# A gated mix of linear attention and a GLU in one kernel: the order of ScalarE's and VectorE's work, denominators in pairs, weight loads behind one another

## The chip, the cores and the metric

One core of a Trainium2 chip runs the whole kernel. The metric is the device time of one execution in microseconds (us); lower is better. TensorE multiplies matrices, ScalarE (ACT in the profile) and VectorE (DVE) work on tiles in SBUF and PSUM, GpSimd (POOL) only issues transfers here, mostly stores, and SyncE (SP) issues all loads. Each of these engines works its own queue of instructions strictly in order: an instruction that waits holds all that stand behind it.

## The reference

```python
def reference(A_x, A_wqkv, A_wo, B_x, B_w_gate, B_w_up, B_w_down, gate_w):
    # x: 2048 tokens x 640, fp32; 32 heads of 20; 1536 features in the GLU
    qkv = (x @ wqkv).reshape(B, S, 3, H, Dh)...
    phi = lambda t: jnp.where(t > 0, t + 1, jnp.exp(t)) + 1e-6
    pq, pk = phi(q), phi(k)
    kv = einsum("bhsd,bhse->bhde", pk, v);  z = einsum("bhsd->bhd", pk)
    num = einsum("bhqd,bhde->bhqe", pq, kv)
    den = einsum("bhqd,bhd->bhq", pq, z) + 1e-6
    a = (num / den).reshape(B, S, D) @ wo
    h = sigmoid(x @ w_gate) * (x @ w_up)
    b = h @ w_down
    g = sigmoid((x * gate_w).sum(-1))
    return g * a + (1 - g) * b
```

All inputs and outputs are fp32.

## The kernel before

**Products.** Every fp32 operand is held as a high and a low part (`split`: ScalarE copies the high part, VectorE subtracts it for the low one), and `mm3` (L214 to L216) issues three matmuls for one product, most of them 128x128 by 128x512. The helpers through which nearly all of ScalarE's and VectorE's work goes have one line each: `act` L225, `vec2` L229, `vec3` L233. So a row of the profile is told apart by its tiles.

**Stages.** First come keys and values, summed over all tokens (0 to about 144 us), then the heads' matrices (`kv_part`, `m_part`) and phi(q) for the second half of the tokens (`q_phase(1)`, to about 206). `f_phase(1)` runs the GLU's twelve feature blocks, f = 0 to 11, for the second half (to 442.5). `q_phase(0)` and `f_phase(0)` do the same for the first half (to about 742). An output stage follows, in which numerators, gate and the parts from the GLU meet (to the end). Blocks of two by two are multiplied with seven products in place of eight (`Block`, steps s1 to s7). The sums of weights this needs are made once, in the second half, on VectorE from a staged tile wst (`queue_g`, `queue_s`, L1052 to L1098), split into wg, wu and ws, stored to DRAM by POOL (`store_w`, L943) and loaded again in the first half by SP (`load_form`, L1018). Some steps start from a product that is already there: a seed, ScalarE's copy of a tile ch in PSUM into a tile dd, after which TensorE adds to dd.

**What sets the order.** The program is written out by hand, with a planner, `Order`. It keeps clocks in us for TensorE, ScalarE and VectorE (`order.pe`, `order.act`, `order.vec`), which each helper moves on by a price: for ScalarE `a_cost(w)` and for VectorE `v_cost(w)`, w the columns of a tile. Work that has no fixed place is put in lists (`order.add`, with prices, a key, a time `ready` before which it isn't taken, and a rank: first, plain, lazy, chain or spare). `fill`, called between products, takes what `_fits`: an item whose end, by the planner's clocks, isn't later than TensorE's clock by more than a slack (0.6 us ScalarE, 1.2 VectorE; 1.6 and 2.4 in q_phase). `order.need(key)` forces an item. The clocks decide only where an instruction stands in its engine's queue; on the chip semaphores make it wait. `W_AT` says when a staged weight is taken to have landed. In `s_part` ws is split in two pieces, each of which needs its part of `sums`.

**Denominators.** phi(q), weighted, is stored by POOL to p_dram while q is made (L1160). `queue_den(g)` (L1196 to L1247) treats one group g of 512 tokens: SP loads five tiles pden (L1208), VectorE sums them with weights zcol into fac (L233), POOL stores the sum (L1218), SP loads it turned (L1224) and the gate's values gs (L1226), VectorE adds twice, takes the reciprocal (L1234) and multiplies by gs, POOL stores the factor (L1236), and SP loads it turned back (L1241). VectorE scales numerators by fac in the output stage, groups 2 and 3 first, then 0 and 1; the scaled tile hf is split into pq for TensorE.

**The GLU's second product.** Two feature blocks make a pair p. Its h is brought into seven forms (B11, B12, B21, B22, T1 to T4; `tail_s` and `queue_h` order them), and multiplied by forms of w_down. Those are made in the second half (`queue_d`, `queue_ds`, `queue_df`) and come back in the first half as one tile wf of 2304 KB, loaded in three pieces (`load_wf`, L1425), wf's tile being single.

**Tiles.** `c_tile` and `h_tile` give out tiles from rings, by turn: "c" tiles, "cx" tiles (which come out of the ring t of four), hf tiles of three pools. A tile given out again makes its new writer wait for the last reader, a store included.

The functions that the change touches follow.

Of the kernel before, what the change touches and what calls it, by code (L numbers as in the profile page):

```python
# [29 lines left out]
class Order:  # L30
# [25 lines left out]
    def follow(self, v, fn, key=None):  # L56

        self.soon.append((self.act, v, fn, key))
# [28 lines left out]
    def _fits(self, it):  # L87
        a, v, fn, key, ready = it
        if ready is not None and self.pe < ready():
            return False  # L90
        end_a = self.act + a
        end = max(self.vec, end_a if a else 0.0) + v
        return not ((a and end_a > self.pe + self.slack_a) or (v and end > self.pe + self.slack_v))
# [64 lines left out]
    def _after(self, after):  # L158
        t = 0.0
        if "p" in after:  # L160
            self.fill()
            t = self.pe
        if "a" in after:
            t = max(t, self.act)
        if "v" in after:
            t = max(t, self.vec)
# [12 lines left out]

def v_cost(w):  # L180
    return 0.155 + w * 0.00104

@with_exitstack
def gated_mix_kernel(ctx: ExitStack, tc: tile.TileContext, xt, xn, wk, wv, wo, wst_q, wst_f, out_t):
# [57 lines left out]
    def split(hi, lo, src, after=""):  # L242
        act(hi, src, AF.Copy, after)
        at = order.act
# [18 lines left out]
    gs = common.tile([P, P], F32, name="gs")  # L263
# [12 lines left out]
    common.tile([P, 64], F32, name="space")  # L276

# [6 lines left out]
    xst = kp.tile([P, 2, KC, CW], F32, name="xst")  # L284

# [419 lines left out]
    def k_split(i, after=""):  # L705
        r = KR.pop(i)
        ph, pl = op_tile("pkh"), op_tile("pkl")
        vh, vl = (t[:, :D].rearrange(view2, j=2) for t in (ph, pl))
        act(vh, r, AF.Copy, after, bias=EPS)
        at = order.act  # L710
# [127 lines left out]
    for c in range(1, 4):  # L838
# [135 lines left out]
        for u in range(2 * KC):  # L974
            g.part(u, 2 if u in g.ps else 0, 4)
            order.fill()
            if u in (3, 5, 7, 9,):
                order.run("qw")
# [21 lines left out]

    def tt(name, dt=F32, shape=(P, TG)):
        return pw.tile(list(shape), dt, name=name, tag="t", bufs=4)
# [19 lines left out]
    WST, W_AT = {}, {}  # L1022
# [173 lines left out]
    def queue_den(g, place=None):  # L1196

        st = {}
        td = fac[:, g]

        def load(u):
            if u < KC:
                if not place:
                    st[u] = tt("pden")
                elif u % 2 == 0:
                    t = place(F32)
                    st[u], st[u + 1] = t[:, 0], t[:, 1]
                nc.sync.dma_start(st[u], p_dram[:, u, g])  # L1208
                st["at", u] = max(order.pe, order.vec) + 9.0

        def one(u):
            if u == 0:
                vec1(td, st[u], zcol[:, 0:1], zeps[:, 0:1], OP.mult, OP.add)
            else:
                vec3(td, st[u], zcol[:, u:u + 1], td, OP.mult, OP.add)
            load(u + 2)
            if u == KC - 1:
                nc.gpsimd.dma_start(den_dram[:, g], td)  # L1218
                st["at", u + 1] = max(order.pe, order.vec) + 7.0

        def turn_in():
            for j in range(4):
                js = slice(j * H, (j + 1) * H)
                nc.sync.dma_start(td[js].rearrange("h (d c) -> h d c", c=P),  # L1224
                                  den_dram[:, g, j * P:(j + 1) * P].rearrange("(d h) c -> h d c", h=H))
            nc.sync.dma_start(gs, gate_rep[4 * g:4 * g + 4].rearrange("i h c -> (i h) c"))  # L1226
            st["at", KC + 1] = max(order.pe, order.vec) + 7.0

        def factor():
# [5 lines left out]
            vec2(q, q, gs, OP.mult)  # L1235
            nc.gpsimd.dma_start(fac_dram[:, g], q)  # L1236
            st["at", KC + 2] = max(order.pe, order.vec) + 7.0

        def turn_out():
            for d in range(4):  # L1240
                nc.sync.dma_start(td[d * H:(d + 1) * H].rearrange("h (j c) -> h j c", c=P),  # L1241
                                  fac_dram[:, g].rearrange("(j h) c -> h j c", h=H))
        order.add(0, 0, lambda: [load(0), load(1)], chain=True)
        for u in range(KC):
            order.add(0, v_cost(TG), lambda u=u: one(u), None, lambda u=u: st["at", u], chain=True)
        for n, (v, fn) in enumerate(((0, turn_in), (2.0, factor), (0, turn_out))):
            order.add(0, v, fn, ("fac", g) if n == 2 else None, lambda n=n: st["at", KC + n], chain=True)  # L1247
# [108 lines left out]
    def load_d():  # L1356
        if d_loads:
# [3 lines left out]
            DST[n] = (t, order.pe + 4.0)  # L1361
# [15 lines left out]
    def queue_ds(p):  # L1377
# [16 lines left out]
        for part in range(2):  # L1394
            order.add(0, 2 * v_cost(2 * P), lambda part=part: sums(part), lazy=True)

    def queue_df(p):
# [16 lines left out]
        for j in range(2):  # L1414
            order.add(a_cost(w), v_cost(w), lambda j=j: forms(j), ("ds", p), lazy=True)
# [4 lines left out]
    def load_wf(p):  # L1420
# [3 lines left out]
        for c0, c1 in ((0, D), (D, 2 * D), (2 * D, WF)):  # L1424
# [17 lines left out]
    def queue_d(n):  # L1442
        if not down_pool:
# [3 lines left out]
                  lazy=True)  # L1447
# [86 lines left out]
    def h_tile(dt=F32R):  # L1534

        i, last = 0, 4
        if "h" in turn:
            last = 3 if "c" in turn else 4
            i = (turn["h"] % 8 >= 4) + (turn["h"] % 8 >= 4 + last)
            turn["h"] += 1  # L1540
        return down_pool[i].tile([P, 2, TG], dt, name="hf", tag=f"hf{i}", bufs=(4, last, 1)[i])
# [40 lines left out]
    def tail_s(f, blk):  # L1582
# [17 lines left out]
        def t5():  # L1600
# [123 lines left out]
    def q_phase(pr, b12, extra):  # L1724
# [9 lines left out]
        for j, (u, b) in enumerate(steps):  # L1734
            if isinstance(u, Block):
# [23 lines left out]
                if pr:  # L1759
# [7 lines left out]
                    elif blk is A and s == 6:  # L1767
                        queue_g(("f", pr, 0))
                    elif blk is A and s == 7:
                        queue_s(("f", pr, 0))  # L1770
                else:
# [19 lines left out]
    dens = ({0: 2, 2: 3, 4: 0, 6: 1}, {})  # L1791

    def f_phase(pr, q, hooks={}):
# [3 lines left out]
        if pr:  # L1797
            turn.update(c1=0, c22=0, h=0)

        def step(f, s):  # L1800
# [6 lines left out]
            if pr and s == 1:  # L1807
                order.need(("w", n, 0), False)
# [22 lines left out]
            if pr:  # L1831
                if s == 7 and f + 2 < FC:
                    queue_s(("f", pr, f + 2))
                if s == 2 and f + 1 < FC:
                    queue_g(("f", pr, f + 1))
                    if f == 0:
                        queue_s(("f", pr, 1))
# [4 lines left out]
        next(q, None)  # L1842
        step(0, 1)
# [3 lines left out]
        for f in range(FC):  # L1847
            if f % 2:
                order.need(("h", f // 2 - 1, "T3"), False)
            down = iter(())  # L1850
            if f % 2 and f > 1:
# [11 lines left out]
            for s in (3, 4, 5):  # L1863
                step(f, s)
                next(down, None)
                if pr and s == 4:
                    if f < 2 or f % 2:
                        queue_d(("f", 1, f))
                    if f % 2 and f < FC - 1:
                        queue_ds(f // 2)  # L1870
            if f + 1 < FC:
# [5 lines left out]
            if f % 2 and f < FC - 1:  # L1877
                if not pr and f > 1:
                    load_wf(f // 2)
                queue_t1(f // 2)  # L1880
                if pr:
                    queue_df(f // 2)
# [4 lines left out]
            if f in dens[pr]:  # L1887
                queue_den(dens[pr][f])
            step(f, 7)
        if pr:  # L1890
# [46 lines left out]
    extra[13].append(lambda: order.need(("w", ("f", 1, 0), 0), False))  # L1937
    for hg, (j, t) in enumerate(((1, "rot"), (2, "rot"), (3, "dd"), (5, "rot"), (6, "rot"), (8, "rot"))):
# [421 lines left out]
```

## Time and profile before

| | before |
|---|---|
| three executions | 803.31, 803.03, 801.63 us |
| median | 803.03 us |
| the profiled execution | 808.18 us, of which the span is 806.0 |
| mean granted TensorE clock | 0.972 |
| moved by DMA | 173.53 MB, mean 215 GB/s |

The profile comes from one execution of its own, 5.2 us above the median, and its rows are held against its own time. "busy" counts from an instruction's start to its end; successive instructions of one engine overlap, so the distance from start to start (the pitch) is shorter than the duration. "[1.51 <-ACT dd L225]" says that the engine stood idle 1.51 us ahead of that instruction, and that ScalarE's writing of dd ended the idle time. PEclk is the share of its full clock that TensorE was granted. A DMA row gives the time of its issue on the queue, and "us to landing" the median from issue to landing.

### The profile page before, as it was taken

The page shows a single profiled execution, that of the slowest core. Times are in us where ns is not written, and L with a number is a line of the kernel's source. Part 1 is how long each engine was busy: PE and PEld are TensorE (multiplying, and loading weights), DVE is VectorE, ACT ScalarE, POOL GpSimd, SP SyncE. Part 2 cuts the span into 40 slices and gives each one's busy share as a digit, 9 for nine tenths or more (in the row PEclk, how much of TensorE's full clock was granted, in tenths as well). Part 3 has the DMA queues.
Part 4 walks back from the last instruction along what each step waited for, and adds up shares of the span by engine and source line. Part 5 has one row for each costly group of instructions (what it writes and reads, how often), then busy time and mean ns, then how long its engine had stood idle before and what let it go on. Part 6 is the DMA issues. An engine that isn't in the chain of part 4 may idle for free.

```text
span 806.0 us, 10081 instructions
## 1 busy us (share of the span) xinstructions
PE 750.3 (93%) x3575; PEld 628.8 (78%) x3575; DVE 568.2 (71%) x987; ACT 357.8 (44%) x661; POOL 94.6 (12%) x161
## 2 busy tenths in 40 slices
PE   9999999997989899988988999999999899998398
PEld 8999999785776777766766888888888688886276
DVE  5978879785676887878869832636767466894496
ACT  6665474476447543434354454354142314231251
POOL 0220201032112110111110210000001300000000
PEclk9999999998999999999999999999999899999589
DMA  7564566985856745554846558849785947494212
GB/s 267 133 186 112 150 182 162 279 295 181 313 191 238 284 156 197 229 208 173 344 177 251 182 196 314 317 149 347 252 325 180 266 174 301 167 349 145 85 65 93
DMA packets 71000, 173.53 MB, mean 215 GB/s; under 512 B 11642, under 2 KB 32394, under 8 KB 67238
## 3 DMA queue, kind: packets, MB, share of 16 engines
q1 hardware_dynamic: 54582, 109.99, 41.2%
q0 software_dynamic: 16224, 62.74, 21.8%
q8 instruction: 28, 0.46, 0.2%
q14 instruction: 22, 0.18, 0.1%
q10 hardware_dynamic: 144, 0.16, 0.1%
HBM read 103.96 MB, written 63.92 MB: 208 GB/s over the span
## 4 chain that ended last, share of the span: by engine, by line
PE 64%; DVE 11%; DMA 10%; issue 9%; ACT 4%; SPq 1%; POOL 1%; DVEq 0%; POOLq 0%; ACTq 0%
PE ch L214 6%; PE ch L216 6%; PE ch L215 6%; PE cc L216 6%; PE cc L215 5%; PE cc L214 5%; PE dd L214 5%; PE dd L216 5%; PE dd L215 5%; PE rot L214 4%; PE rot L215 4%; PE rot L216 4%; DMA ws<-wf 2%; DVE tb L229 1%; DVE hf L229 1%
## 5 line engine op out<-in xcount | busy, mean ns | idle before, releaser
L229 DVE TENSOR_TENSOR hf<-c,hf 128x512 fp32r<-128x512 f32 x74 | 50.7, 689 | 48.9 <-ACT hf L225 47.8
L225 ACT ACTIVATE c<-ch 128x512 f32<-128x512 f32 x50 | 29.8, 595 | 98.6 <-PE ch L216 98.5
L225 ACT ACTIVATE hf<-c 128x512 fp32r<-128x512 f32 x74 | 46.0, 626 | 48.5 <-DVE c L229 48.2
L214 PE MATMUL ch<-xth,ws 128*128 128x512 f32 x112 | 44.8, 400 | 7.0 <-DMA ws<-wf 3.9
L229 DVE TENSOR_TENSOR c<-cc,c 128x512 f32<-128x512 f32 x38 | 26.2, 690 | 35.2 <-PE cc L216 18.5
L214 PE MATMUL dd<-xrh,wg 128*128 128x512 f32 x90 | 36.3, 403 | 12.6 <-ACT dd L225 12.6
L216 PE MATMUL ch<-xth,ws 128*128 128x512 f32 x112 | 44.6, 398 | 0.0
L215 PE MATMUL ch<-xtl,ws 128*128 128x512 f32 x112 | 44.5, 398 | 0.0
L229 DVE TENSOR_TENSOR tb<-rot,tb 128x512 f32<-128x512 f32 (+1 forms) x59 | 38.2, 676 | 6.3 <-PE rot L216 5.4
L229 DVE TENSOR_TENSOR tb<-dd,tb 128x512 f32<-128x512 f32 x44 | 30.2, 687 | 13.4 <-PE dd L216 13.3
L216 PE MATMUL dd<-xrh,wg 128*128 128x512 f32 x90 | 35.9, 399 | 0.0
L215 PE MATMUL dd<-xrl,wg 128*128 128x512 f32 x90 | 35.7, 397 | 0.0
L214 PE MATMUL cc<-xbh,ws 128*128 128x512 f32 x84 | 33.5, 399 | 0.0
L215 PE MATMUL cc<-xbl,ws 128*128 128x512 f32 x84 | 33.3, 396 | 0.0
L216 PE MATMUL cc<-xbh,ws 128*128 128x512 f32 x84 | 33.2, 395 | 0.0
L229 DVE TENSOR_TENSOR c<-c,c 128x512 f32<-128x512 f32 x44 | 30.1, 685 | 2.4 <-ACT c L225 2.0
L214 PE MATMUL rot<-pkh,xnh 128*128 128x320 f32 x102 | 31.6, 310 | 0.0
L215 PE MATMUL rot<-pkl,xnh 128*128 128x320 f32 x102 | 31.5, 309 | 0.0
L214 PEld LDWEIGHTS dd<-xrh,wg 128*128 128x128 f32 x90 | 17.1, 190 | 18.5 <-ACT dd L225 15.1
L216 PE MATMUL rot<-pkh,xnl 128*128 128x320 f32 x102 | 31.5, 308 | 0.0
L225 ACT ACTIVATE ws<-wst 128x640 fp32r<-128x640 f32 (+1 forms) x26 | 17.4, 679 | 30.7 <-DVE wst L229 17.9
L214 PEld LDWEIGHTS ch<-xth,ws 128*128 128x128 f32 x112 | 21.4, 191 | 12.2 <-DMA ws<-wf 4.3
(649 smaller groups left out, 2341.7 us busy)
## 6 DMA issues: line engine op xcount, KB each, us to landing
wf<-ws POOLq DMA_DIRECT2D x12, 1152.0 KB, 7.5
ws<-wf SPq DMA_DIRECT2D x12, 1152.0 KB, 8.2
wst<-wst_f SPq DMA_DIRECT2D x12, 640.0 KB, 6.9
wf<-wg POOLq DMA_DIRECT2D x12, 640.0 KB, 7.5
wd<-wd POOLq DMA_DIRECT2D x12, 640.0 KB, 7.7
wg<-wf SPq DMA_DIRECT2D x12, 640.0 KB, 4.0
wf<-wd SPq DMA_DIRECT2D x10, 640.0 KB, 5.8
xnst<-xn SPq DMA_DIRECT2D x16, 320.0 KB, 4.5
```

Of the source, the lines that this page charges most:

```text
L214: nc.tensor.matmul(out, l_hi, r_hi, start=first, stop=False, skip_group_check=True)
L215: nc.tensor.matmul(out, l_hi, r_lo, start=False, stop=False, skip_group_check=True)
L216: nc.tensor.matmul(out, l_lo, r_hi, start=False, stop=last, skip_group_check=True)
L225: nc.scalar.activation(out, src, fn, **kw)
L229: nc.vector.tensor_tensor(out, a, b, op=op)
```

## The change

The program keeps its instructions: ScalarE, VectorE, SP, POOL and TensorE have as many as before, and TensorE's matmuls stand in the same order, but for the PSUM banks of the last batch of GT. What differs is where the others' instructions stand in their queues, and which tiles some of them use.

1. Prices: one for ScalarE and one for VectorE, lower than before, and lags of 0.2, 0.18 and 0.14 us where one engine reads what TensorE, ScalarE or VectorE wrote.

```diff
-        self.act = max(self.act, t) + 0.19 + w * 0.00084
+        self.act = max(self.act, t) + a_cost(w)
...
-        self.vec = max(self.vec, t) + 0.155 + w * 0.00104 * rate
+        self.vec = max(self.vec, t) + v_cost(w * rate)
+
+P_LAG, A_LAG, V_LAG = 0.2, 0.18, 0.14
 
 def a_cost(w):
-    return 0.19 + w * 0.00084
+    return 0.06 + w / 1200
 
 def v_cost(w):
-    return 0.155 + w * 0.00104
+    return 0.07 + w / 960
```

2. The split of ws isn't taken before its sums are through by VectorE's clock, and the weights of f + 1 are queued a step or more earlier (`queue_g` and `queue_s` of f = 0 and 1 within `q_phase`), and forced at step 7 of the block before.

```diff
+            SUM_AT[n, 1 - part] = order.vec + V_LAG
...
+            order.act = max(order.act, SUM_AT[n, part])
             split(h[:, cs], l[:, cs], WST[n][:, part, :cut[part + 1] - cut[part]])
...
-                order.add(a_cost(w), v_cost(w), lambda part=part: s_part(part), ("w", n, part))
+                order.add(a_cost(w), v_cost(w), lambda part=part: s_part(part), ("w", n, part),
+                          lambda part=part: SUM_AT.get((n, part), 1e9))
...
-            if pr and s == 1:
-                order.need(("w", n, 0), False)
+            if pr and s == 7 and f + 1 < FC:
+                for part in range(2):
+                    order.need(("w", ("f", 1, f + 1), part), False)
```

3. Denominators of two groups together, item by item in turn: groups 2 and 3 from f = 3 of `f_phase(0)` on, groups 0 and 1 from f = 7. Each group's gs has a tile of ring t. The work per group is the same.

```diff
-    dens = ({0: 2, 2: 3, 4: 0, 6: 1}, {})
+    dens = ({3: (2, 3), 7: (0, 1)}, {})
...
-    def queue_den(g, place=None):
+    def queue_dens(*gs2):
...
+        order.add(0, 0, lambda: [load(g, u) for u in range(2) for g in gs2], chain=True)
         for u in range(KC):
-            order.add(0, v_cost(TG), lambda u=u: one(u), None, lambda u=u: st["at", u], chain=True)
+            for g in gs2:
+                order.add(0, v_cost(TG), lambda g=g, u=u: one(g, u), None, lambda g=g, u=u: st["at", g, u], chain=True)
```

4. `load_wf(f // 2)` moves from behind step 1 of the next block to behind step 7, which puts it behind that step's load of ws on SP's queue; its pieces come in another order, the one that is used first in front.

```diff
-        for c0, c1 in ((0, D), (D, 2 * D), (2 * D, WF)):
+        for c0, c1 in ((D, 2 * D), (0, D), (2 * D, WF)):
...
-                if not pr and f > 1:
-                    load_wf(f // 2)
                 queue_t1(f // 2)
...
             step(f, 7)
+            if not pr and f % 2 and 1 < f < FC - 1:
+                load_wf(f // 2)
```

5. Forms of h: B22 is queued first, and T3 = B22 - B12 is made behind it; T4 and T3 are queued only at step 3 of the next odd block. The turns c1, c22 and h begin in `f_phase(1)` after q_phase's first step there in place of ahead of it, so that `q_phase(1)` takes "c" tiles where it took "cx" tiles. The last hf tile of eight comes from another pool.

```diff
-        if pr:
-            turn.update(c1=0, c22=0, h=0)
...
         next(q, None)
+        if pr:
+            turn.update(c1=0, c22=0, h=0)
         step(0, 1)
...
-            queue_h(p, "B22")
-            queue_h(p, "T4")
-            HR[p, "T3"] = t3 = HR.pop((p, "B12"))
-            queue_h(p, "T3", lambda: sub(t3, HR[p, "B22"], t3))
+            HR[p, "T3"] = t3 = HR[p, "B22"]
+            b12 = HR.pop((p, "B12"))
+
+            def b22():
+                h_form(p, "B22")
+                order.then(lambda: sub(t3, t3, b12))
+            order.add(a_cost(TG), 2 * v_cost(TG), b22, ("h", p, "B22"), first=True)
...
+                if s == 3 and f % 2 and f > 1:
+                    queue_h(f // 2 - 1, "T4")
+                    queue_h(f // 2 - 1, "T3")
```

6. Smaller: the first w_down forms are no longer lazy (`lazy=p > 0`, `lazy=n[2] > 1`), `DST`'s landing is taken at 10 us in place of 4, and the last GT batch takes the banks rot, dd, rot, cc in turn.

More of the change, by code (lines that the diff above doesn't have):

```diff
@@ L243, in split @@
         act(hi, src, AF.Copy, after)
-        at = order.act
+        at = order.act + A_LAG
         def low():
@@ L709, in k_split @@
         act(vh, r, AF.Copy, after, bias=EPS)
-        at = order.act
+        at = order.act + A_LAG
         def low():
@@ L999, in gated_mix_kernel @@
     pw2 = pw2_cm.__enter__()
+    pw2.tile([P, 2, D], F32, name="wst", tag="wst", bufs=2)
+    pw2.tile([P, 2, TG], F32R, name="hf", tag="hf2")
+    pw2.tile([P, 256], F32, name="room")
     def tt(name, dt=F32, shape=(P, TG)):
@@ L1194, in gate_store, with load, one, turn_in @@
         nc.sync.dma_start(gate_rep, gate_dram[0].rearrange("(i o p) -> i o p", o=1, p=P).broadcast_to([n, H, P]))
[L1196 removed]
+    def queue_dens(*gs2):
         st = {}
[L1199 to L1201 removed]
+        def load(g, u):
             if u < KC:
[L1203 to L1211, printed above, removed]
+                st[g, u] = tt("pden")
+                nc.sync.dma_start(st[g, u], p_dram[:, u, g])
+                st["at", g, u] = max(order.pe, order.vec) + 9.0
+        def one(g, u):
+            td = fac[:, g]
             if u == 0:
[L1213 removed]
+                vec1(td, st[g, u], zcol[:, 0:1], zeps[:, 0:1], OP.mult, OP.add)
             else:
[L1215 to L1216 removed]
+                vec3(td, st[g, u], zcol[:, u:u + 1], td, OP.mult, OP.add)
+            load(g, u + 2)
             if u == KC - 1:
                 nc.gpsimd.dma_start(den_dram[:, g], td)
[L1219 to L1221 removed]
+                st["at", g, u + 1] = max(order.pe, order.vec) + 7.0
+        def turn_in(g):
             for j in range(4):
                 js = slice(j * H, (j + 1) * H)
[L1224 removed]
+                nc.sync.dma_start(fac[js, g].rearrange("h (d c) -> h d c", c=P),
                                   den_dram[:, g, j * P:(j + 1) * P].rearrange("(d h) c -> h d c", h=H))
[L1226 to L1229 removed]
+            st[g, "gs"] = tt("gs")[:, :P]
+            nc.sync.dma_start(st[g, "gs"], gate_rep[4 * g:4 * g + 4].rearrange("i h c -> (i h) c"))
+            st["at", g, KC + 1] = max(order.pe, order.vec) + 7.0
+        def factor(g):
+            td = fac[:, g]
             q = td[:, :P]
@@ L1394, in queue_ds @@
         for part in range(2):
-            order.add(0, 2 * v_cost(2 * P), lambda part=part: sums(part), lazy=True)
+            order.add(0, 2 * v_cost(2 * P), lambda part=part: sums(part), lazy=p > 0)
     def queue_df(p):
@@ L1534, in h_tile @@
     def h_tile(dt=F32R):
-        i, last = 0, 4
+        i = 0
         if "h" in turn:
-            last = 3 if "c" in turn else 4
-            i = (turn["h"] % 8 >= 4) + (turn["h"] % 8 >= 4 + last)
+            i = (0, 0, 0, 0, 1, 1, 1, 2)[turn["h"] % 8]
             turn["h"] += 1
-        return down_pool[i].tile([P, 2, TG], dt, name="hf", tag=f"hf{i}", bufs=(4, last, 1)[i])
+        pool = pw2 if i == 2 and "c1" in turn else down_pool[i]
+        return pool.tile([P, 2, TG], dt, name="hf", tag=f"hf{i}", bufs=(4, 3, 1)[i])
     def h_split(f, g, src, after):
@@ L1848, in f_phase @@
             if f % 2:
-                order.need(("h", f // 2 - 1, "T3"), False)
+                order.need(("h", f // 2 - 1, "B22"), False)
             down = iter(())
+            if f in dens[pr]:
+                queue_dens(*dens[pr][f])
             if f % 2 and f > 1:
```

53 lines of the change are left out of this document (28 added, 25 removed).

## The prediction

> **What bounds the kernel now.** I read the page's busy times first, then stretches of the span, then who TensorE waits for, then the places themselves.
>
> ```profile
> PE 750.3 (93%) x3575; PEld 628.8 (78%) x3575; DVE 568.2 (71%) x987; ACT 357.8 (44%) x661; POOL 94.6 (12%) x161
> ```
>
> TensorE is the bound, but 93% hides where it is idle or slow. Stretches of the span (columns: us; length, then busy us and instructions of PE, PEld, DVE, ACT, POOL; granted clock, DMA share, GB/s):
>
> ```profile
> 144.00:190.00 46.00, 42.59 (x232) 36.05 (x231) 33.82 (x68) 28.65 (x55) 10.45 (x19) 1.00 0.88 290
> 190.00:206.00 16.00, 11.65 (x39) 8.50 (x38) 9.22 (x16) 9.47 (x16) 3.31 (x7) 0.79 0.59 197
> 206.00:442.50 236.50, 215.03 (x899) 168.33 (x897) 181.92 (x316) 108.35 (x195) 35.88 (x63) 0.99 0.61 227
> 442.50:633.00 190.50, 190.32 (x842) 156.92 (x843) 113.12 (x176) 78.19 (x134) 22.08 (x40) 1.00 0.72 254
> 633.00:643.00 10.00, 6.14 (x17) 4.57 (x16) 1.38 (x2) 1.70 (x3) 2.88 (x5) 0.66 1.08 226
> ...
> 742.00:772.00 30.00, 12.82 (x32) 9.18 (x31) 16.30 (x26) 7.10 (x13) 1.08 (x2) 0.61 0.24 83
> 772.00:801.00 29.00, 28.10 (x129) 22.53 (x129) 25.91 (x48) 12.35 (x24) 0.00 (x0) 1.00 0.22 80
> 500.00:600.00 100.00, 100.00 (x442) 82.36 (x441) 61.22 (x94) 42.15 (x75) 3.78 (x7) 1.00 0.76 278
> ```
>
> In 500 to 600 TensorE never stops: 442 matmuls in 100 us, a pitch of 0.2262 us. Length less count times pitch is what a stretch loses to idle time and to half clock together: 190 to 206 loses 16.0 - 8.8 = 7.2; 206 to 442.5 (feature blocks of the second half of the tokens, f_phase(1)) 236.5 - 203.4 = 33.1; 442.5 to 633 nothing; 633 to 643 10.0 - 3.8 = 6.2; 742 to 772 30.0 - 7.2 = 22.8. Where 256-wide matmuls mix in I take the idle time alone: 3.4 in 144 to 190, 0.9 in 772 to 801. About 74 us in all. Whom TensorE waits for (us in total, times, longest):
>
> ```profile
> PE dd L214 <- ACT dd L225: 13.8, 8, 3.7
> PE dd L214 <- DVE dd L229: 11.5, 1, 11.5
> PE cc L214 <- ACT pq L225: 4.5, 1, 4.5
> PE ch L214 <- DMA ws<-wf: 3.9, 1, 3.9
> PE cc L214 <- ACT ws L225: 3.8, 5, 1.2
> PE ch L214 <- ACT c L225: 3.1, 1, 3.1
> PE rot L1318 <- DMA wv_sb<-wv: 1.8, 1, 1.8
> PE dd L214 <- ACT ms L225: 1.3, 1, 1.3
> ```
>
> None of these is work TensorE lacks time for: each is a short operation that came late. The matmuls stay as many and in the same order, so only such lateness can change.
>
> **Step 1: the order of ScalarE and VectorE (costs, lags, SUM_AT; 206 to 442.5).** One of the eight dd waits:
>
> ```profile
> 316.71 1.08 DVE L229 TENSOR_TENSOR wst<-wst 128x256 f32<-128x256 f32 x3
> 317.87 0.74 ACT L225 ACTIVATE ws<-wst 128x640 fp32r<-128x640 f32 x1 [2.49 <-issue]
> 318.51 0.58 ACT L225 ACTIVATE dd<-ch 128x512 f32<-128x512 f32 x1
> 319.15 0.50 PE L214 MATMUL dd<-xrh,wg 128*128 128x512 f32 x1 [1.51 <-ACT dd L225]
> ```
>
> ScalarE idles 2.49 us at the head of its queue, because the split of ws stands there and VectorE's sums of wst end only at 316.71 + 1.08 = 317.79. Behind it stands the copy that seeds dd. Its source, counted in the order of instructions, was complete nine matmuls (2.0 us) before the last one ahead of the gap, so ScalarE, free since 317.87 - 2.49 = 315.38, could have made it. TensorE loses 1.51. With SUM_AT the split is not put in the queue before its sums are through by the planner's clock. In the changed order the seed stands ahead of the split here, some 2 us earlier than it ran, more than the wait. So the waits on ACT dd and ACT ws go: 13.8 + 3.8 less the 1.2 of one that lies before 206 = 16.4. The clock of 0.99 over 236.5 us is another 2.4. That bounds the gain below: 33.1 - 18.8 = about 14 left. Above, the small waits alone stay, some 2 us. The other 12 us are VectorE coming late, which hangs on whether the new prices are truer:
>
> ```profile
> L229 DVE TENSOR_TENSOR hf<-c,hf 128x512 fp32r<-128x512 f32 x74 | 50.7, 689 | 48.9 <-ACT hf L225 47.8
> 716.75 3.09 DVE L229 TENSOR_TENSOR pq<-pl,pq 128x512 fp32r<-128x512 f32 x5
> 719.76 0.68 DVE L229 TENSOR_TENSOR bl<-bl,omg 128x512 f32<-128x512 f32 x1
> 763.77 2.18 ACT L225 ACTIVATE pq<-hf 128x512 fp32r<-128x512 f32 x4
> 765.85 0.58 ACT L225 ACTIVATE bl<-rot 128x512 f32<-128x512 f32 x1
> ```
>
> The old prices of 512 columns, 0.687 for VectorE and 0.620 for ScalarE, are durations (VectorE's mean is 689 ns). Back to back, five VectorE operations take 719.76 - 716.75 = 3.01, 0.602 each; four on ScalarE 2.08, 0.52 each. The new prices are 0.603 and 0.487, with a lag to the reader apart. VectorE's is exact, ScalarE's 0.03 short, which 195 operations in 236 us at 46% busy can bear. After the gain VectorE is busy 181.9 of about 208 us, so it has some 26 us of room, and not every small wait will go. I take 5 left: gain 28.1, ends 19.1 and 31.1.
>
> The Trainium skill speaks against these pitches. "VectorE: DVE Perf Modes", section "The DRAIN you can't avoid", says that the next operation does not start until the pipeline is empty, which would make the pitch the duration; its next sentence lets an operation that is not held start earlier. The trace shows 0.602 against 0.689, so the second holds here.
>
> **Step 2: c1, c22 and h turns, tiles of the q phase (190 to 206).**
>
> ```profile
> 191.93 0.60 ACT L225 ACTIVATE qr<-ch 128x512 f32<-128x512 f32 x1 [1.70 <-DMA p_dram<-qe]
> 194.49 0.58 ACT L225 ACTIVATE c<-ch 128x512 f32<-128x512 f32 x1
> p_dram<-qe POOLq DMA_DIRECT2D x20, 256.0 KB, 4.6
> ```
>
> ScalarE waits 1.70 at 191.93 for a store of qe, because the ring of tiles comes round too soon; the copy c<-ch, for which TensorE waits 3.1, is held behind it. With the turns set after the q phase has begun, that phase takes other tiles, and a tile's store is 36 matmuls (8.1 us) before its next use, against 9 (2.0 us). The store lands in 4.6, with some 3.5 to spare. The wait and the stretch's low clock (0.21 of 16 = 3.4) go together. Of 7.2 I leave 1.5 for the ws wait of 1.2 and a rest: gain 5.7, ends 3.5 and 7.2. In 144 to 190 the waits for wv_sb and ms (1.8 + 1.3) stay; 0.4, ends 0 and 0.4. Before 144 nothing is counted; other banks for one GT batch take none away.
>
> **Step 3: weight loads (633 to 643).**
>
> ```profile
> 615.18 2.18 SPq L1425 DMA_DIRECT2D wf<-wd  x3
> 621.30 0.32 SPq L1018 DMA_DIRECT2D ws<-wf  x1
> 637.37 0.79 PE L214 MATMUL ch<-xth,ws 128*128 128x512 f32 x1 [3.86 <-DMA ws<-wf]
> ws<-wf SPq DMA_DIRECT2D x12, 1152.0 KB, 8.2
> wf<-wd SPq DMA_DIRECT2D x10, 640.0 KB, 5.8
> ```
>
> ws is issued 6 us behind three pieces of wf (2304 KB) and TensorE waits 3.86 for it, 16 us after its issue, then runs at 0.66. The change queues wf after ws. ws then has 55 matmuls (12.4 us) against a median of 8.2. The wait moves to wf: its distance from issue to first use falls from 88 matmuls (19.9 us) to 61 (13.8). Ahead of and with its first piece lie 1152 + 640 KB, 1.83 MB, 7.2 us at the stage's 254 GB/s; the two medians one after the other are 14.0, 0.2 too much. I take the rate, since a median holds what was queued ahead. Left 1.5, gain 4.7, ends 0 and 6.2.
>
> **Step 4: dens in pairs (742 to 801, and what it costs before).**
>
> ```profile
> fac<-fac_dram SPq DMA_DIRECT2D x16, 64.0 KB, 6.3
> 751.39 0.75 DVE L229 TENSOR_TENSOR fac<-fac 128x256 f32<-128x256 f32 x2 [6.35 <-DMA fac<-den_dram]
> 753.37 0.69 DVE L229 TENSOR_TENSOR dd<-bl,omg 128x512 f32<-128x512 f32 x1
> 754.12 0.79 PE L214 MATMUL dd<-pq,ws 128*128 128x512 f32 x1 [11.48 <-DVE dd L229]
> 759.02 0.69 DVE L233 SCALAR_TENSOR_TENSOR hf<-hf,fac 128x512 f32<-128x512 f32 x1 [4.96 <-DMA fac<-fac_dram]
> ```
>
> The last group's denominators are summed in the output stage itself: load, sum, store, turn, reciprocal, store, turn, with the head of VectorE's queue waiting 6.35 and 4.96 for the turns. Behind it stands dd<-bl,omg, for which TensorE waits 11.48, and then the pq copies (4.5). In the changed order the last factor is made after matmul 3024, and its first reader is behind matmul 3264: 240 matmuls, 54 us, for a last turn of 6.3 in step 3's queue. The hf loads there have 220 matmuls (49.8 us). Of 22.8 + 0.9 I leave 2.0 for a first tile or two: gain 21.7; ends 23.7, and 15.7 if one wait like 4.5 stays with 3.4 of half clock, as in 190 to 206.
>
> The cost lies in f_phase(0), 442.5 to 742. The 20 pden loads now go in pairs, four in flight, on SP's queue.
>
> ```profile
> 737.26 0.75 DVE L233 SCALAR_TENSOR_TENSOR fac<-pden,zcol,fac 128x512 f32<-128x512 f32 x1 [3.94 <-DMA pden<-p_dram]
> ```
>
> The worst is the last of them in feature block 9: queued behind ws and wf, 3.46 MB (13.6 us at 254 GB/s), and read by VectorE 36 matmuls (8.1 us) after its issue. VectorE stands still for some 5.5 us; behind it is the sum c12, on which through ScalarE TensorE depends 91 matmuls (20.6 us) after the issue. Some 2.5 us are left; in feature block 3 some 1.7. Both could fail, so I take 1.5 us lost, ends 0 and 15 (about four waits of 3.94).
>
> What a new wait would cost beyond itself: in 206 to 442.5 waits up to 3.7 left the clock at 0.99, in 742 to 772 one of 11.48 brought it to 0.61. "TensorE: Matmul & The Clock Gate", Part 1 of the Trainium skill, halves the rate after an idle window of about 3.4 us that runs free; by it one new wait near that length would make 1.5 into about 5.
>
> **Sum.** 28.1 + 5.7 + 0.4 + 4.7 + 21.7 - 1.5 = 59.1 us off the profiled execution's own 808.2 (span 806.0 and 2.2 around it): 749.1. It lies 5.2 above the median of 803.03. If that excess is spread evenly, the median becomes 743.9; if it sits in waits that vanish, 749.1. I say 746. All good ends (68.6) give 734, all bad ones (23.3) 780.
>
> **Rivals.** (a) Only the named waits of step 1 go, VectorE stays late: 9 us less, 755; with steps 3 and 4's output stage at their bad ends too (4.7 + 6.0), 766. For: a busy VectorE in 206 to 442.5; against: the pitches. 15%. (b) Duration is the true price: the planner puts too much in, and all 28.1 of step 1 stay lost: 774. The Trainium skill's drain is this case. Against: 0.602 is measured over five operations. 7%. (c) wf is late in all four places that are moved, each at 633's price of 6.2: 24.8 less the 1.5 already left, 769. For: 14.0 against 13.8 by medians; against: the rate. 6%. (d) The slower side: VectorE's queue stops for pden all through f_phase(0), since a load behind weights on SP's queue holds all behind it. At 3.94 each, 20 loads make 79, in place of step 4's 1.5: 746 - 1.5 + 79 = 823. From 15 loads on it outweighs the gain (803.0 - 744.5 = 58.5). For: VectorE did wait so at 737.26; against: in 442.5 to 633 loads of pden cost TensorE nothing, and pairs have four under way where there were two. 8%. (e) The order comes out much as before: 803. 2%.
>
> **How the numbers follow.** Forecast 62%, the rest as said. My own case spans 734 to 755; (a) reaches 766, and with (c) I go to 770, which leaves out (b), (d) and (e), 17%. A difference under 0.2% can't be told from none in this kernel. Faster 90%, same 2% (e), slower 8% (d).
>
> **What would show it.** Step 1: dd <- ACT dd falls from 13.8 to under 3, and 899 matmuls fit in some 208 us. Step 2: no wait of 3.1 on ACT c, no ACT wait on p_dram<-qe over 1. Step 3: no wait on ws<-wf, and none on wf<-wd. Step 4: no VectorE wait on fac<-den_dram near the end, and the clock near 1.00 there. Wrong would be new TensorE waits of 2 us and more between the feature blocks of f_phase(0) while VectorE waits for pden, or waits for wf four times.

## The result, and the profile after

The changed kernel takes 739.79 us (median of four runs, 738.43 to 740.67) against 803.13 us (801.63 to 803.31): a ratio of 0.9214, 95% interval 0.9195 to 0.9232. Forecast were 746, between 734 and 770.

The page of the changed kernel, its span and the busy times:

```profile
span 737.6 us, 10091 instructions
...
PE 729.6 (99%) x3575; PEld 621.3 (84%) x3575; DVE 563.7 (76%) x987; ACT 354.5 (48%) x661; POOL 95.2 (13%) x161
```

Each engine has as many counted instructions as before (the first line also counts semaphore instructions, of which there are ten more). TensorE's busy time is 20.7 us less, largely because the half clock is gone (the mean granted clock was 0.972), and its idle time 47.7 us less (55.7 to 8.0). The same stretches as in the prediction, cut where the same matmuls of the trace stand (columns as there):

```profile
144.50:188.70 44.20, 42.71 (x233) 36.09 (x231) 33.83 (x69) 28.97 (x55) 11.96 (x21) 1.00 0.87 296
188.70:198.10 9.40, 8.95 (x40) 7.10 (x39) 7.77 (x14) 6.53 (x10) 2.35 (x5) 1.00 0.97 377
198.10:405.30 207.20, 206.03 (x899) 167.52 (x898) 178.50 (x313) 107.00 (x195) 36.47 (x65) 1.00 0.70 256
405.30:596.40 191.10, 190.73 (x844) 156.71 (x843) 118.40 (x186) 76.86 (x134) 15.45 (x29) 1.00 0.77 261
596.40:599.80 3.40, 3.40 (x17) 2.81 (x15) 0.14 (x1) 1.57 (x3) 0.00 (x0) 1.00 1.04 405
599.80:698.70 98.90, 98.90 (x436) 81.21 (x435) 83.03 (x133) 34.24 (x64) 10.88 (x19) 1.00 0.74 245
698.70:705.70 7.00, 7.00 (x32) 5.81 (x31) 6.93 (x16) 4.98 (x10) 0.00 (x0) 1.00 0.20 75
```

The granted clock is 1.00 everywhere. Worked out from the start of the same matmuls in both traces:

| stretch before (us) | before | after | gain | forecast |
|---|---|---|---|---|
| 0 to 144 | 143.2 | 143.7 | -0.5 | 0 |
| 144 to 190 | 46.0 | 44.2 | 1.8 | 0.4 |
| 190 to 206 | 16.1 | 9.4 | 6.7 | 5.7 |
| 206 to 442.5, f_phase(1) | 236.6 | 207.2 | 29.4 | 28.1 |
| 442.5 to 633 | 190.4 | 191.1 | -0.7 | with the next two |
| 633 to 643 | 9.9 | 3.4 | 6.5 | 4.7 |
| 643 to 742 | 99.0 | 98.9 | 0.1 | these three: 3.2 |
| 742 to 806 | 63.9 | 38.9 | 25.0 | 21.7 |

The gains add up to 68.3 us, and the spans differ by 68.4 (806.0 less 737.6). Who still makes TensorE wait:

```profile
PE dd L216 <- ACT ms L227: 1.2, 2, 0.9
PE rot L302 <- PEq L2371: 0.8, 1, 0.8
PE ch L216 <- ACT c L227: 0.8, 2, 0.5
PE ch L216 <- ACT ws L227: 0.4, 1, 0.4
PE cc L216 <- DVE tb L231: 0.4, 1, 0.4
...
PE dd L216 <- ACT dd L227: 0.2, 1, 0.2
```

The largest is 1.2 us over two waits; ACT dd, 13.8 over eight before, is down to 0.2.

### The profile page after: what moved, and what is told of

Its sections match the earlier page's. It is cut to its first block, busy times and chain, and to the rows that moved or that the text cites. A ratio compares the mean times of both kernels' runs of the same rounds, so it can differ in the third digit from the quotient of the medians.

```text
span 737.6 us, 10091 instructions
## 1 busy us (share of the span) xinstructions
PE 729.6 (99%) x3575; PEld 621.3 (84%) x3575; DVE 563.7 (76%) x987; ACT 354.5 (48%) x661; POOL 95.2 (13%) x161
## 4 chain that ended last, share of the span: by engine, by line
PE 89%; issue 3%; DMA 3%; ACT 2%; DVE 1%; POOL 1%; POOLq 0%; ACTq 0%
PE ch L218 9%; PE ch L216 9%; PE ch L217 9%; PE cc L216 8%; PE cc L218 7%; PE cc L217 7%; PE dd L216 7%; PE dd L217 7%; PE dd L218 7%; PE rot L216 6%; PE rot L217 6%; PE rot L218 6%; DMA wo_sb<-wo 1%; DMA wd<-ds 1%; ACT c L227 0%
## 5 line engine op out<-in xcount | busy, mean ns | idle before, releaser
L216 PE MATMUL ch<-xth,ws 128*128 128x512 f32 x112 | 44.2, 394 | 1.1 <-ACT c L227 0.5
L218 PE MATMUL ch<-xth,ws 128*128 128x512 f32 x112 | 43.7, 391 | 0.1
L231 DVE TENSOR_TENSOR tb<-dd,tb 128x512 f32<-128x512 f32 x44 | 30.1, 685 | 10.5 <-PE dd L218 10.5
L216 PE MATMUL dd<-xrh,wg 128*128 128x512 f32 x90 | 35.1, 390 | 0.0
L218 PE MATMUL dd<-xrh,wg 128*128 128x512 f32 x90 | 35.0, 389 | 0.0
L231 DVE TENSOR_TENSOR c<-c,c 128x512 f32<-128x512 f32 x46 | 31.6, 686 | 2.6 <-ACT c L227 2.0
L231 DVE TENSOR_TENSOR wst<-wst 128x256 f32<-128x256 f32 (+2 forms) x69 | 27.4, 412 | 1.4
L216 PE MATMUL rot<-pkh,xnh 128*128 128x320 f32 x90 | 28.0, 311 | 0.0
L217 PE MATMUL rot<-pkl,xnh 128*128 128x320 f32 x90 | 27.8, 309 | 0.0
L218 PE MATMUL rot<-pkh,xnl 128*128 128x320 f32 x90 | 27.8, 309 | 0.0
L227 ACT ACTIVATE c<-dd 128x512 f32<-128x512 f32 x22 | 13.0, 592 | 29.3 <-PE dd L218 26.2
```

The costliest lines, as they stand in the source:

```text
L216: nc.tensor.matmul(out, l_hi, r_hi, start=first, stop=False, skip_group_check=True)
L217: nc.tensor.matmul(out, l_hi, r_lo, start=False, stop=False, skip_group_check=True)
L218: nc.tensor.matmul(out, l_lo, r_hi, start=False, stop=last, skip_group_check=True)
L227: nc.scalar.activation(out, src, fn, **kw)
L231: nc.vector.tensor_tensor(out, a, b, op=op)
```

## Experiments

All stretches below are cut at the same matmuls. A kernel named a_ starts from the changed one (739.8), b_ from the one before (803 to 805 beside it on the same chip). Ratios are to the kernel before. A stretch is read from one execution of each kernel; the one from 144 to 190 took 42.0 to 47.6 us among the kernels named a_, so a difference of 2 us there says little.

### What carries step 1: the gate or the prices?

a_no_sumat takes the gate away:

```diff
-            order.act = max(order.act, SUM_AT[n, part])
...
-                order.add(..., ("w", n, part), lambda part=part: SUM_AT.get((n, part), 1e9))
+                order.add(..., ("w", n, part))
```

> The changed kernel without SUM_AT: the split of ws may be queued ahead of its sums again; prices, lags and all else as changed. Theory of the prediction (step 1, SUM_AT takes the split from in front of the seeds, worth the waits on ACT dd and ACT ws with their half clock): the stretch of f_phase(1), 207 us in the changed kernel, grows by 16 to 19 us, about 757 in all. Rival (the lower prices and the earlier queueing already put the sums far enough ahead; the gate is worth little): at most 3 us more, 740 to 743. Where both hold in part, several waits on ACT dd come back but not eight.

740.33 us, ratio to before 0.9205 (0.9148 to 0.9262); f_phase(1) takes 206.9. Its stretch in a_no_sumat (columns as above):

```profile
201.60:408.40 206.80, 205.65 (x898) 167.70 (x897) 178.49 (x312) 107.08 (x195) 36.06 (x64) 1.00 0.70 255
```

The gate is worth nothing here, and what the prediction called the cause is not it. In the changed kernel, timeline of one split of ws:

```profile
301.28 0.74 ACT L227 ACTIVATE ws<-wst 128x640 fp32r<-128x640 f32 x1 [2.48 <-DVE wst L231]
301.92 0.58 ACT L227 ACTIVATE c<-dd 128x512 f32<-128x512 f32 x1
```

ScalarE stands at the split and waits 2.48 us for the sums there, just as it did at 317.87 before. TensorE doesn't notice, since no seed stands behind it.

a_old_prices puts the old prices back, without lags; a_old_pitch does so with the new lags:

```diff
-P_LAG, A_LAG, V_LAG = 0.2, 0.18, 0.14
+P_LAG, A_LAG, V_LAG = 0.0, 0.0, 0.0     (a_old_prices alone)
...
-    return 0.06 + w / 1200
+    return 0.19 + w * 0.00084
...
-    return 0.07 + w / 960
+    return 0.155 + w * 0.00104
```

> The changed kernel with the old prices (0.62 and 0.69 us at 512 columns) and no lags; SUM_AT, queueing, pairs and loads as changed. Theory of the prediction (prices are worth the rest of step 1, VectorE coming late): f_phase(1) grows by 9 to 12 us, about 750. Rival one (prices are all of step 1): by 25 to 30 us, about 768. Rival two (prices only set how much slack the planner believes in, and the items stand in the same places): under 2 us, 740 to 742.

> The changed kernel with the old prices and the new lags, to part the two. If the prices carry the 35 us: 770 to 780. If the lags carry them (an operation that reads another engine's result is placed too early without them): under 745. If each carries a part: between.

775.27 us (0.9642, 0.9593 to 0.9692) and 781.73 us (0.9738, 0.9689 to 0.9787). f_phase(1) takes 234.8 and 240.0: nearly all of its gain is gone. The lags don't carry it; with dear prices they make it worse. Whether they earn anything beside the new prices was not tried. a_old_prices loses 6.4 us more from 190 to 206, and 4.7 from 643 to 742, about the start of which VectorE waits 6.0 us for a load of pden. Yet these are mostly not the old waits. Whom TensorE waits for in a_old_prices:

```profile
PE rot L216 <- DVE tb L231: 4.9, 4, 2.0
PE rot L216 <- ACT ds L227: 4.8, 3, 2.4
PE ch L216 <- ACT ws L227: 3.6, 2, 3.2
PE dd L216 <- ACT wd L227: 3.5, 1, 3.5
```

ACT dd is gone (in a_old_pitch it is back with 6.2 us in four), and splits of weights (ds, ws, wd, wg) have come in its place. One of them, ACT, DVE and PE rows of a_old_prices:

```profile
328.02 0.60 ACT L227 ACTIVATE cx<-ch 128x512 f32<-128x512 f32 x1 [4.18 <-PE ch L218]
329.26 0.87 DVE L231 TENSOR_TENSOR dst<-dst 128x256 f32<-128x256 f32 x2
329.71 1.15 ACT L227 ACTIVATE ds<-dst 128x512 fp32r<-128x512 f32 x2 [1.09 <-DVE dst L231]
...
330.39 0.50 PE L216 MATMUL rot<-hf,ds 128*128 128x512 f32 x1 [2.41 <-ACT ds L227]
```

ScalarE stood idle 4.18 us until ch was there, copied it, stood idle 1.09 us more until VectorE's sums of dst, and only then did the split of ds for which TensorE waited. In three feature blocks of a_old_prices a split of ds ends 0.1 us before its reader. In the changed kernel the same one, ACT and PE rows, is done 24 us ahead:

```profile
289.16 1.16 ACT L227 ACTIVATE ds<-dst 128x512 fp32r<-128x512 f32 x2 [1.14 <-DVE dst L231]
...
313.86 0.39 PE L216 MATMUL rot<-hf,ds 128*128 128x512 f32 x1
```

The reading of this: at 0.62 and 0.69 us an operation the planner believes the engines full, so work without a fixed place is put off until it is forced. a_old_prices_slack, below, tests it.

### Where the seeds' waits come from

a_need_early undoes one line of queueing:

```diff
-            if pr and s == 7 and f + 1 < FC:
-                for part in range(2):
-                    order.need(("w", ("f", 1, f + 1), part), False)
+            if pr and s == 1:
+                order.need(("w", n, 0), False)
```

> The changed kernel with one line of queueing undone: the first part of ws of f + 1 is forced at its step 1 again, in place of both parts at step 7 of the block before, which comes three steps later. Theory now (the waits on ACT dd come from this forcing: need takes the item whatever its ready time, the split goes into ScalarE's queue ahead of its sums and the seed stands behind it): five or six waits on ACT dd of 1.5 to 3.7 us come back, f_phase(1) grows from 207 to 222 to 232 us, 755 to 765 in all. Rival (prices and SUM_AT are enough, the sums are made early whoever forces the split): under 3 us more, 740 to 743.

769.45 us (0.9575, 0.9517 to 0.9633), f_phase(1) 236.0, more than was expected. The waits on ACT dd are back. Their row in a_need_early, and the timeline of one of them, DVE, ACT and PE rows:

```profile
PE dd L216 <- ACT dd L227: 12.3, 7, 4.2
```

```profile
308.43 2.00 DVE L231 TENSOR_TENSOR wst<-wst 128x256 f32<-128x256 f32 x5
310.47 0.74 ACT L227 ACTIVATE ws<-wst 128x640 fp32r<-128x640 f32 x1 [3.35 <-DVE wst L231]
311.11 0.58 ACT L227 ACTIVATE dd<-ch 128x512 f32<-128x512 f32 x1
311.74 0.62 PE L216 MATMUL dd<-xrh,wg 128*128 128x512 f32 x1 [2.38 <-ACT dd L227]
```

It is the picture of 317.87 again, with SUM_AT and the new prices in place: `need` takes the split whatever its ready time says, and the sums with it, and puts the seed behind both. What took the split from in front of the seed was the forcing three steps later, an edit that the prediction's sum gave no price.

b_prices gives the kernel before the new prices and lags alone, b_prices_need the new place of the forcing too (the diff above, turned round):

> The kernel before with the new prices and lags alone: old queueing, no SUM_AT, single denominators, wf ahead of ws. If prices alone are step 1, f_phase(1) falls from 236.6 to 207 to 212 us; with some 4 us more before it and the output stage unchanged, 770 to 776. If they work only together with the earlier queueing and the forms that are no longer lazy, f_phase(1) stays above 222 and the whole above 785.

> The kernel before with the new prices and lags and with the forcing moved to step 7; still no SUM_AT, single denominators, old turns, old place of wf. With the prices alone f_phase(1) took 230.3 us and the whole 791. Theory now (step 1 is the product of two things, prices and the place of the forcing): f_phase(1) falls to 207 to 212 us, 768 to 774 in all. Rival (SUM_AT or the queueing in q_phase is needed too): f_phase(1) stays above 218, above 779.

791.44 us (0.9869, 0.9833 to 0.9905) and 783.07 us (0.9740, 0.9672 to 0.9808); f_phase(1) takes 230.3 and 220.3. Who holds TensorE there, a row of b_prices, then one of b_prices_need:

```profile
PE dd L216 <- ACT dd L227: 14.7, 6, 3.0
```

```profile
PE ch L216 <- ACT ws L227: 7.2, 5, 1.6
```

In b_prices_need ACT dd is no longer among the waits. So the prices and lags alone earn 6.3 us of 29.4, with the new place of the forcing 16.3, and 13.1 need something else that came with the change (the earlier queueing of the weights, the order of h forms, the tiles' turns, w_down's first forms no longer lazy, dst's landing taken at 10 us); which of these was not tried. In both runs the pessimistic expectation held, in the second by its numbers alone: whether SUM_AT or the queueing in q_phase is what it lacked is open.

a_old_prices_slack asks whether dear prices hurt only by putting work off; the old prices stay, and fill gets more room:

```diff
-        self.slack_a, self.slack_v = (1.6, 2.4) if long else (0.6, 1.2)
+        self.slack_a, self.slack_v = (3.6, 4.4) if long else (2.6, 3.2)
```

> The changed kernel with the old prices and no lags (775), and with every slack of fill 2 us larger. Theory now (dear prices make the planner believe ScalarE and VectorE full, so that items that have time are put off until they are forced one matmul before their use, while the engines stand idle): the larger slack lets them in, f_phase(1) falls from 234.8 to 207 to 216 us, 740 to 752. Rival (what counts is the true order among the engines, which only right prices give): f_phase(1) stays above 225, above 765.

779.09 us (0.9696, 0.9641 to 0.9751), slower than a_old_prices. f_phase(1) gains 7.8, to 227.0, and the wait on ds falls from 4.8 to 1.2. But 11.8 us are lost in the stretch from 442.5 to 633 (169.8 less 158.0 in its second part), where nothing was lost before. DVE and PE rows there:

```profile
603.26 1.23 DVE L242 TENSOR_SCALAR fac<-pden,zcol,zeps 128x512 f32<-128x512 f32 x2 [7.51 <-DMA pden<-p_dram]
...
606.09 0.80 PE L216 MATMUL rot<-hf,wf 128*128 128x512 f32 x1 [9.66 <-DVE tb L231]
```

The larger slack let a sum of pden into VectorE's queue too soon; VectorE waited 7.51 us for the load and TensorE 9.66 behind it. A slack lets everything in; the prices say what there is room for. The rival held here: more room in fill gives back only 7.8 of the 27.6 us that f_phase(1) lost in a_old_prices, so putting work off is at best a part of what dear prices cost.

### Step 2: the turns

```diff
+        if pr:
+            turn.update(c1=0, c22=0, h=0)
         next(q, None)
-        if pr:
-            turn.update(c1=0, c22=0, h=0)
         step(0, 1)
```

> The changed kernel with the turns c1, c22 and h begun ahead of the q phase's first step again, so that q_phase(1) takes cx tiles as in the kernel before. Theory of the prediction (step 2: ScalarE waits for stores of qe because the ring comes round too soon): ScalarE's waits on p_dram<-qe come back, 4 to 6 us in all, and the two stretches from matmul row 948 to 1217 (53.6 us in the changed kernel) grow by 4 to 6 us, about 745. Rival (the old prices made that loss, as they leave 57.8 us there with the turns changed): waits on p_dram<-qe come back but cost under 1.5 us, 740 to 741.

749.29 us (0.9344, 0.9312 to 0.9375), 9.5 more than the changed kernel; the two stretches from 144 to 206 take 63.2 in place of 53.6 (before, 62.1). ACT and PE rows of a_turn_early:

```profile
193.80 0.60 ACT L227 ACTIVATE qr<-ch 128x512 f32<-128x512 f32 x1 [7.77 <-DMA p_dram<-qe]
...
198.37 0.58 ACT L227 ACTIVATE c<-ch 128x512 f32<-128x512 f32 x1
...
199.01 0.79 PE L216 MATMUL ch<-xth,ws 128*128 128x512 f32 x1 [8.41 <-ACT c L227]
```

The ring of tiles is the cause, as forecast: ScalarE waits 7.77 for the store, and c<-ch behind it makes TensorE wait 8.41. Undone, it costs 9.6. The turns aren't enough by themselves: in a_old_prices, which has them and no wait for a store of qe, the stretch from 190 to 206 takes 15.8 us in place of 9.4, and TensorE waits 3.2 us there for ACT c and 1.3 for the split of wg.

### Steps 3 and 4: who held ws, and what the pairs earn

a_wf_early puts `load_wf` back in front of ws in the changed kernel (below). b_wf_late moves it behind ws in the kernel before, with the new order of its pieces:

```diff
-            if not pr and f % 2 and 1 < f < FC - 1:
-                load_wf(f // 2)
...
+                if not pr and f > 1:
+                    load_wf(f // 2)
                 queue_t1(f // 2)
```

> The changed kernel with wf loaded ahead of ws again (behind step 1 of the next block); the new order of its pieces stays. Theory of the prediction (ws was late because it was queued behind 2304 KB of wf): the wait on ws<-wf comes back in feature block 9 with its half clock, about 6 us, 746. Rival (the 16 gathers from m_dram on POOL's queue crowded the DMA engines in that stretch; the pairs have moved them behind the denominators' stores, which come later): no wait on ws<-wf, under 1.5 us, 740 to 741.

> The kernel before with wf alone moved behind step 7, pieces in the new order; the 16 gathers on POOL's queue stay where they were. If the place in SP's queue is enough by itself: no wait on ws<-wf in feature block 9, that stretch 3.4 us in place of 9.9, about 797, and none on wf<-wd. If the gathers crowd the DMA engines whatever the queue: a wait of 2 to 5 us stays there, on ws<-wf or on wf<-wd, 800 to 805.

739.93 us (0.9204, 0.9155 to 0.9252) and 806.26 us (1.0032, 1.0006 to 1.0059). With wf in front the wait on ws is 1.1 us, not 3.9, and the stretch 4.9 us, not 9.9; in the time it doesn't show. And moved alone it gains nothing: the stretch falls from 9.9 to 4.6, and the next (643 to 742) grows from 99.0 to 104.6. In b_wf_late loads of pden stand behind ws and wf on SP's queue, and one issued at 629.42 landed at 644.73. VectorE's row there:

```profile
644.75 0.55 DVE L240 TENSOR_SCALAR fac<-pden,zcol,zeps 128x512 f32<-128x512 f32 x1 [5.40 <-DMA pden<-p_dram]
```

That wait of 5.40 is the slower rival of the prediction on a small scale. What else stood beside ws before is on POOL's queue. Timeline of POOL in the kernel before, and in b_pairs, where the pairs alone are changed:

```profile
621.48 0.62 POOL L1463 DMA_DIRECT2D mt<-m_dram  x1 [0.20 <-PE cc L216]
622.53 3.43 POOL L1463 DMA_DIRECT2D mt<-m_dram  x6 [0.43 <-issue]
```

```profile
636.41 0.55 POOL L1213 DMA_DIRECT2D den_dram<-fac  x1 [14.05 <-DVE fac L233]
637.16 0.62 POOL L1463 DMA_DIRECT2D mt<-m_dram  x1 [0.21 <-PE dd L216]
638.23 3.42 POOL L1463 DMA_DIRECT2D mt<-m_dram  x6 [0.44 <-issue]
```

Sixteen gathers (the heads' matrices in rows of 512 bytes) were issued from 621.48 on, 0.2 us after ws. The opening says that SyncE issues all loads; these sixteen GpSimd issues. In b_pairs they stand behind a store of den_dram that waits for the second pair's sums, 4 us after the stretch's first matmul.

> The kernel before with the denominators in pairs alone; wf still ahead of ws, old prices. Theory now (the pairs earn the output stage, and also the wait on ws<-wf, since the gathers on POOL's queue stand behind the second pair's stores): the output stage from matmul row 3405 on takes 38 to 42 us in place of 64.0, the stretch at feature block 9 3.4 to 5 in place of 9.9, 770 to 776 in all. Rival one (the wait on ws<-wf needs wf behind ws): that stretch stays near 9.9, 776 to 780. Rival two (the pairs make VectorE wait for pden in f_phase(0), the slower side of the prediction): more than 5 us lost between matmul row 2262 and 3405 beside it.

b_pairs takes 775.79 us (0.9658, 0.9600 to 0.9716). The stretch at 633 takes 4.7 with wf still in front, and the output stage 38.9 in place of 63.9; between the two nothing is lost (99.0). The first part of the output stage in b_pairs, which took 30.1 us before:

```profile
737.00:744.00 7.00, 7.00 (x32) 5.81 (x31) 6.88 (x15) 3.66 (x9) 0.00 (x0) 1.00 0.20 75
```

So the pairs take away the wait on ws as well. But they aren't its only cure: b_prices, with wf in front and the gathers 0.2 us after ws as before, waited only 0.9 us for ws (4.6 for the stretch), and b_prices_need, issued alike, 2.8. The pairs, the prices and wf's place each brought the stretch to 4.6 or 4.7 alone. The gathers fit the long wait but don't suffice for it, and what made it 3.9 us before stays open.

a_dens_single is the other way round, one group at a time in the changed kernel, queued where they were before and with gs in a tile of its own again:

```diff
-    dens = ({3: (2, 3), 7: (0, 1)}, {})
+    dens = ({0: (2,), 2: (3,), 4: (0,), 6: (1,)}, {})
```

> The changed kernel with the denominators one group at a time again, at f = 0, 2, 4, 6, as in the kernel before (gs in a tile of its own, zpart over zsum to make room); prices, SUM_AT and loads as changed. Theory of the prediction (step 4: the last group slips into the output stage because groups are worked one after another): the output stage's first 30 us come back, 22 to 25 us more, about 763; in feature block 9 the gathers stand earlier too, which may add up to 6. Rival (with the lower prices the groups would end in time by themselves): under 5 us, 740 to 745.

766.94 us (0.9547, 0.9496 to 0.9599): the output stage takes 61.9, and 4.8 us are lost in 643 to 742, by the same VectorE wait for pden as in b_wf_late (4.10 us at 611.22). The last group ends in the output stage whatever the prices.

None of the twelve was faster than the changed kernel.

## Why the prediction was right, and where its reasons were not

The direction was right, and the sizes of steps 1 to 4 were within 3.3 us. The sum came out 9.2 us too small because nearly every place did better than was taken: 1.3 us in step 1, 1.0 in step 2, 1.4 from 144 to 190, 2.7 in step 3 with the cost of step 4, and 3.3 in step 4; 0.5 was lost ahead of 144. From 144 to 190 the wait of 1.8 us for wv_sb, which was to stay, is gone; why was not tried.

Step 1, size right (28.1 against 29.4), cause wrong. "With SUM_AT the split is not put in the queue before its sums are through", with 18.8 us hung on it, fails: without SUM_AT the stretch takes 206.9. The seeds' waits hang on the place of the forcing, which had no term. The reading of the gap itself (a split that waits for its sums, with the seed behind) was right, as a_need_early shows. The split of the gain into 19 for order and 9 for prices fails too. Undo the prices and lags and 27.6 us are lost, undo the forcing and 28.8; give the old kernel the prices and lags and 6.3 are won, with the forcing 16.3. Such terms don't add: either one undone is enough to lose nearly all. That the size came out near is no merit of the cause: it came from 899 matmuls at 0.2262 us each, 203.4, and a remainder of 5 (3.8 stayed), which holds for whatever takes the lateness away. As far as the forecast relied on SUM_AT, it was luck that the same change moved the forcing.

Rival (b), duration as the true price, is refuted: with durations as prices f_phase(1) takes 234.8, with pitches 207.2. That VectorE's pitch (0.602) is below its duration (0.689) agrees with the Trainium skill, by which an operation that isn't held starts earlier ("VectorE: DVE Perf Modes", "The DRAIN you can't avoid").

Step 2 was right in cause, and near in size: 6.7 where 5.7 were taken. It left out that this stretch needs the new prices too (15.8 us in a_old_prices, 16.1 before).

Step 3: the term was near (6.5 against 4.7), its cause at most half right. Moving wf took the wait on ws away in b_wf_late, but gave the time back a few us later, and in the changed kernel wf's place is worth nothing in the median (1.5 us in the stretch). The gathers on POOL's queue, beside ws and not in front of it, had no place in the prediction, which looked at SP's queue alone. That the term came near is luck.

Step 4 was right in cause: 25.0 against 21.7, and 25.0 again in b_pairs. It passes the good end of 23.7, since 2.0 us came from 772 to 801, where 0.9 had been counted. The cost in front of it came as a wait of VectorE, 4.47 us for pden in feature block 9 (5.5 had been worked out, from 3456 KB taken as 3.46 MB; by the measure that step 3 uses they are 3.54 MB, and the wait 5.8), and TensorE lost nothing by it:

```profile
599.66 0.75 DVE L235 SCALAR_TENSOR_TENSOR fac<-pden,zcol,fac 128x512 f32<-128x512 f32 x1 [4.47 <-DMA pden<-p_dram]
```

Rival (d) did not happen in the changed kernel, but its mechanism is real: VectorE waited 5.40, 4.10, 7.51 and 6.0 us for one load in four experiments.

The 5.2 us by which the profiled execution of before lay above its median are gone too (739.57 against 739.79), so the median fell by 63.3 where the profiled time fell by 68.6. So the second way of carrying it over held, by which the sum gave 749.1; that 746, halfway, came 3 us nearer is luck.

## What to carry to other kernels

A planner that places work by clocks should be fed the pitch at which operations follow one another: here prices a sixth too dear cost 27.6 us in one stage, with work that came late while the engines idled, and a larger slack didn't make up for it. Forcing an item ahead of the thing it needs costs whatever stands behind it in that queue, so look for the forced item before the gate. And undo parts one at a time before crediting them: lateness doesn't add up, and a move that looks like the cure of a wait (wf behind ws) may be paid for elsewhere or be done already by another.

## What the runs showed of the hardware that was not expected

Half clock came after a short wait. In b_prices_need TensorE waited 1.61 us at 355.61, and from 357 to 360 the granted clock was 0.55; within 353.4 to 357 it had been busy 1.86 of 3.6 us. PE row, then the two stretches:

```profile
355.61 0.50 PE L216 MATMUL ch<-xth,ws 128*128 128x512 f32 x1 [1.61 <-ACT ws L227]
```

```profile
353.40:357.00 3.60, 1.86 (x7) 0.96 (x6) 2.76 (x7) 2.33 (x5) 0.00 (x0) 1.00 0.00 0
357.00:360.00 3.00, 3.00 (x9) 2.34 (x8) 2.27 (x5) 1.82 (x4) 1.07 (x2) 0.55 0.58 123
```

The prediction used "TensorE: Matmul & The Clock Gate", Part 1, of the Trainium skill as a rule for waits near 3.4 us. Here the clock fell behind a stretch of about that length in which TensorE was idle for half the time and never longer than 1.61 us at once; it is one place, and what share of idle time it takes was not measured. In a_need_early, with seven waits on ACT dd of up to 4.2 us, the clock over f_phase(1) was 0.96, where eight waits of up to 3.7 had left 0.99 before, though TensorE was idle about as long in both (20.5 and 21.5 us).
